# Moving the attention backward ahead of the gate and up weight gradients, with streamed operands and earlier end work, in a one-core transformer-block gradient kernel

## Chip, cores and metric

One core of one Trainium2 chip. The metric is the device time of one execution in microseconds (us); lower is better. A ratio is the mean time of one kernel's fast runs over that of the other's fast runs of the same rounds on the same chip, so it is not quite the ratio of the medians that are also quoted. A difference counts as faster or slower when its 95% interval lies outside 2%.

Two kinds of number are used: the timed runs (several executions of each kernel), and one profiled execution of each kernel, from which the stages are read. Profiled times are called spans. Engines: PE is TensorE's matmuls, PEld its weight loads, DVE is VectorE, ACT is ScalarE, POOL is GpSimd, SP issues the loads.

## The reference

The kernel computes the output of a transformer block and all its gradients in one pass. S = 2048 tokens, D = 512, 32 heads of 16, F = 1792, all bf16.

```python
def _A_ref(x, wqkv, wo):            # sliding local attention, window 8, dilation 2
    qkv = ...                        # (x @ wqkv) split into q, k, v by heads
    idx = pos[:, None] - arange(8)[None, :] * 2
    logits = einsum('bhsd,bhswd->bhsw', q, k[idx]) * scale   # masked where idx < 0
    attn = softmax(logits)
    o = einsum('bhsw,bhswd->bhsd', attn, v[idx])
    return o @ wo

def _B_ref(x, w_gate, w_up, w_down):
    return ((x @ w_gate) * (x @ w_up)) @ w_down

mod = silu(c) @ w_mod                # six rows of 512: sa, ca, ga, sb, cb, gb
h = layernorm(x) * (1 + ca) + sa
x = x + ga * _A_ref(h, A_wqkv, A_wo)
h = layernorm(x) * (1 + cb) + sb
x = x + gb * _B_ref(h, w_gate, w_up, w_down)
# outputs: x and the vjp of it for a given grad_out:
#          dx, dwqkv, dwo, dw_gate, dw_up, dw_down, dc, dw_mod
```

## The kernel before

The kernel walks through the block forward and then backward, one stage after the other. Two large buffers (BIG1, BIG2) and two of medium size (M1, M2) are handed from stage to stage; small work tiles come in numbered families `wt(0)` to `wt(5)` with four buffers each. Accumulators come from PSUM pools psA (2), psB (4) and psT (2). All loads are issued on one queue, all stores on another. A scheduler chooses each engine's instruction order from the program. Names: h1 and h2 are the outputs of the two layer norms, dao is the gradient of the attention block's output, oT the attention output before wo (transposed) and d_oT its gradient; dwmod(n) is one of six parts of dw_mod. Only what the change touches is shown.

```python
def store(out_ap, in_ap): nc.gpsimd.dma_start(out=out_ap, in_=in_ap)
def load(out_ap, in_ap):  nc.sync.dma_start(out=out_ap, in_=in_ap)

# --- start: x, the weights, then c; mod = silu(c) @ w_mod; weights are transposed and stored
for q in range(4):
    load(x_tok[:, q * 4:(q + 1) * 4, :], x_dram[:, q * 4:(q + 1) * 4, :])
# ... cut: loads of w_mod, wqkv, w_gate, w_up, w_down, wo
c_bf = sm(0, "c_bf", (P, DC), BF16)
nc.sync.dma_start(out=c_bf[:], in_=c.rearrange("o (dc p) -> p (o dc)", p=P))
# ... cut

def dwmod_chunk(n):                  # one 512x512 part of dw_mod: an outer product
    dmrow = wt(1, "dmrow")
    nc.vector.tensor_copy(out=dmrow[0:1, :], in_=dmodb[0:1, n, :])
    dwm_sb = wbig("dwm_sb")
    dwm3 = dwm_sb[:].rearrange("p (a b) -> p a b", a=DC)
    for dt in range(DC):
        ps = ps_tile(psB, "dwm_ps")
        nc.tensor.matmul(ps[:], lhsT=silu_row[0:1, dt * P:(dt + 1) * P], rhs=dmrow[0:1, :], start=True, stop=True)
        evac(dwm3[:, dt, :], ps[:], eng="s")
    store(out8_v[:, :, n * D:(n + 1) * D], dwm3)

# ... cut: forward, dw_down, dhh, then "dh" with norm-backward 2, which stores dao tile by tile
for n in (2, 3, 4, 5):
    dwmod_chunk(n)

# --- "dw": dw_gate and dw_up, h2 resident (2 MB)
h2_tok = _carve(m1, 0, [NT, D])
load(h2_tok, h2_d[:])
for XT, out_ap in ((DGT, out_4), (DUT, out_5)):
    for fq in range(4):
        fw = min(512, F - fq * 512)          # 512, 512, 512, 256
        nblk = fw // P
        accs = [ps_tile(psB, f"dw_acc{i}") for i in range(3)]
        accs.append(ps_tile(psA, "dw_acc3"))
        for t in range(NT):
            stg = pst_tile([P, 4, P], "stg")
            for j in range(nblk):
                nc.tensor.transpose(out=stg[:, j, :], in_=XT[:, fq * 4 + j, t * P:(t + 1) * P], identity=ident[:])
            stg_sb = wt(3, "stg_sb6", (P, 4, P))
            evac(stg_sb[:, 0:nblk, :], stg[:, 0:nblk, :], eng="v")
            rhs = stg_sb[:, 0:nblk, :].rearrange("p a b -> p (a b)")
            for dt in range(DC):
                nc.tensor.matmul(accs[dt][:, 0:fw], lhsT=h2_tok[:, t, dt * P:(dt + 1) * P], rhs=rhs, start=(t == 0), stop=(t == NT - 1))
        # ... cut: accumulators to SBUF, store

# --- "d_oT": dao transposed, times woT
load(dao_tok, dao_d[:])                      # 2 MB in one load
for t in range(NT):
    transpose_tok_to_T(dao_tok[:, t, :], d_aoT, t)
load(WoT, WoT_d[:])
# ... cut: 64 matmuls into do_ps, copied to d_oT (in BIG1)
# --- "dwo": oT and dao resident, 16 tiles of 4 transposes and 4 matmuls
# --- "dAT": attention weights' gradient; q, k, v resident in BIG2
for half in range(2):
    for htpair in range(2):
        for sc2 in range(2):
            ps = ps_tile(psB, "dat_ps")
            for htlo in range(2):
                for w in range(W):
                    prod = wt(0, "prodA")
                    ew.mul(prod[:], d_oT[...], vT2[...])          # VectorE
                    nc.tensor.matmul(ps[:], lhsT=GselP[:, htlo, w, :], rhs=prod[:], ...)
            evac(dAT[...], ps[:])
    # ... cut: softmax backward on VectorE, 8 tiles
# --- transposes of attention and its gradient (taT_ps), then the "dqkv loop", then:
h1_tok2 = _carve(big1, 0, [NT, D])
wmod2 = _carve(big1, NT * D, [DC, 6 * D])
load(h1_tok2, h1_d[:])                                        # 2 MB
load(wmod2, w_mod.rearrange("(dc p) n -> p dc n", p=P))       # 3 MB
# --- norm-backward 1
for t in range(NT):
    x_l = wt(4, "x_l9")
    load(x_l[:], x_dram[:, t, :])
    dx1_l = wt(5, "dx1_l9")
    load(dx1_l[:], dx1_d[:, t, :])
    # ... cut: dh1, layer norm backward (n_bwd is its first op on x), dx
# --- "dwq": dwqkv, 3 x 16 tiles of 4 transposes (psA) and 4 matmuls (psB)
# ... cut
for n in (0, 1):
    dwmod_chunk(n)
for dc in range(DC):
    nc.vector.tensor_tensor_reduce(out=junk10, in0=wmod2[:, dc, :], in1=dmod_rep, op0=ALU.mult, op1=ALU.add, scale=1.0, scalar=0.0, accum_out=dsilu[:, dc:dc + 1])
# ... cut: dc
```

## Time and profile before

Median 1368.64 us over 6 runs (1364.48 to 1372.37). The profiled execution has a span of 1370.7 us.

The busy line of the profile's page: for each engine the busy us, its share of the span and its instructions.

```profile
...
PE 1129.6 (82%) x5892; PEld 524.5 (38%) x5892; DVE 812.0 (59%) x2217; ACT 557.4 (41%) x1039; POOL 127.6 (9%) x243
...
```

TensorE is the busiest engine, but no engine is busy throughout. The stages follow one another, and each has its own limit. So the question is where TensorE starves. Busy time of each engine in four stretches of the kernel before (window, its length, busy us and instructions of each engine, granted TensorE clock as a share of full speed, DMA share, GB/s):

```profile
core 0: us, PE busy (x) PEld busy (x) DVE busy (x) ACT busy (x) POOL busy (x), PEclk, DMA share, GB/s
755.00:778.00 23.00, 16.80 (x49) 5.61 (x49) 8.12 (x22) 11.63 (x23) 3.35 (x5) 0.55 0.40 144
923.00:933.30 10.30, 0.11 (x2) 0.00 (x0) 0.00 (x0) 1.08 (x4) 0.75 (x1) 0.74 0.91 330
954.00:975.00 21.00, 20.91 (x141) 10.42 (x139) 11.15 (x31) 1.31 (x4) 0.18 (x2) 1.00 0.01 1
977.00:1035.00 58.00, 41.88 (x153) 13.88 (x152) 56.81 (x169) 5.22 (x9) 0.75 (x1) 0.81 0.07 26
...
```

The first stretch is the passage from dh to dw: TensorE is busy 16.80 of 23 us, and its granted clock is 0.55. The second is a stop: TensorE does 0.11 us in 10.3, while the DMA moves 330 GB/s. The third is dwo, with VectorE about half busy. The fourth is dAT with softmax backward: VectorE is busy 56.81 of 58 us.

What the stop waits for stands in the timeline of TensorE of the kernel before (start, busy us, instruction, then in brackets the idle time before it and what ended it):

```profile
...
933.36 3.24 PE L349 MATMUL stg<-ident,m_dao 128*128 128x128 bf16 x24 [10.25 <-DMA m_dao<-dao_d]
...
```

It is the single 2 MB load of dao. Two more waits, from the views of waits of the kernel before (engine, line and tile, what it waited for, total us, times, longest), the first at the start, the second at the start of norm-backward 1:

```profile
...
DVE t L84 <- DMA WgT_d<-wTt: 28.8, 1, 28.8
...
```

```profile
...
ACT n_bwd L627 <- DMA x_l<-in_A_x_dram: 11.3, 1, 11.3
...
```

The layer-norm products t cannot be written until the stored weight transposes have left their shared buffers. And norm-backward 1 waits for its first x tile, because 5 MB (h1 and w_mod) stand in front of it in the load queue.

At the end, the reductions for dc are four long VectorE operations. They are seen in the groups of VectorE instructions of the kernel before from 1289.8 us on (shapes, count | busy us, mean ns | idle):

```profile
...
L916 DVE CUSTOM_DVE_ANT_0 m_p<-big_p,m_p 128x3072 bf16<-128x3072 bf16 x4 | 13.3, 3336 | 0.0
...
```

Where they fall inside dwq, VectorE cannot copy the transposed tiles for TensorE. The waits of that stage, 1289.8 to 1357.0 us:

```profile
...
PE dwq_acc L901 <- DVE stg_sb L62: 12.8, 22, 1.6
...
```

### The profile page before, as it was taken

Reading aid. Unit: us, or ns where it says so; the run is one execution under the profiler, and the core shown is the slowest. Engines: PE = TensorE matmul, PEld = TensorE weight load, DVE = VectorE, ACT = ScalarE, POOL = GpSimd, SP = SyncE. Lnnn points to the kernel's source line nnn. Section 1 sums busy time; section 2 is a strip of 40 time slices with the busy share of each in tenths; the row PEclk is TensorE's granted clock in tenths of the full one; section 3 lists DMA queues with packets and bytes.
Section 4 is the critical chain, followed back from the end, with each engine's and each line's share of the span. In section 5 each row is a group of like instructions: output and inputs, shape, how many; then the busy total and the mean of one; then the engine's idle time right before and its main releaser. Section 6 shows DMA issues by size and latency. Waiting matters only on the chain. (4 is left out here: it accounts for less than half of the span.)

```text
span 1370.7 us, 16900 instructions
## 1 busy us (share of the span) xinstructions
PE 1129.6 (82%) x5892; PEld 524.5 (38%) x5892; DVE 812.0 (59%) x2217; ACT 557.4 (41%) x1039; POOL 127.6 (9%) x243
## 2 busy tenths in 40 slices
PE   1669959975999968798999788887977999978776
PEld 1334423332444434443444345454324334333343
DVE  1445879998445655484444323223796999955751
ACT  1833356751332111163444310112107888857602
POOL 4530000021000130000111100000000000001100
PEclk9858979986999989998999799998978999989998
DMA  9530320053113250203322303213101000042101
GB/s 363 150 116 31 126 95 14 1 215 123 39 35 97 69 188 24 66 1 127 97 93 83 125 32 122 104 50 127 47 0 47 1 1 1 0 177 92 55 16 62
DMA packets 58439, 110.10 MB, mean 80 GB/s; under 512 B 21360, under 2 KB 44400, under 8 KB 56176
## 3 DMA queue, kind: packets, MB, share of 16 engines
q1 hardware_dynamic: 45376, 62.24, 13.5%
q0 software_dynamic: 12976, 46.77, 9.2%
q8 instruction: 46, 0.75, 0.2%
q14 instruction: 41, 0.34, 0.1%
HBM read 62.23 MB, written 46.76 MB: 80 GB/s over the span
## 5 line engine op out<-in xcount | busy, mean ns | idle before, releaser
L62 DVE COPY stg_sb<-stg 128x512 bf16<-128x512 bf16 (+1 forms) x248 | 90.1, 401 | 201.2 <-PE stg L696 102.4
L701 PE MATMUL dw_acc<-stg_sb,m_h2tok 128*128 128x512 bf16 (+1 forms) x512 | 110.1, 357 | 19.9 <-DVE stg_sb L62 17.9
L60 ACT ACTIVATE arep_sb<-arep_ps 128x512 bf16<-128x512 f32 x128 | 76.6, 598 | 13.9 <-PE arep_ps L827 8.9
L701 PEld LDWEIGHTS <-m_h2tok 128*128 128x128 bf16 x512 | 49.7, 98 | 68.7 <-issue 27.1
L60 ACT ACTIVATE dlrep_sb<-dlrep_ps 128x512 bf16<-128x512 f32 x112 | 67.2, 600 | 8.2 <-PE dlrep_ps L831 3.9
L62 DVE CAST big_u<-gu_ps 128x512 bf16<-128x512 f32 x56 | 38.7, 692 | 52.9 <-PE gu_ps L521 52.9
L60 ACT ACTIVATE dw_sb<-dw_acc 128x512 bf16<-128x512 f32 (+1 forms) x32 | 14.8, 550 | 133.6 <-issue 116.0
L312 PE MATMUL stg<-ident,big_p 128*128 128x128 bf16 x232 | 31.5, 289 | 45.2 <-DMA big_p<-in_A_wqkv_dram 20.8
L580 PE MATMUL dwd_ps<-m_dffn,stg_sb 128*128 128x512 bf16 x224 | 55.0, 390 | 14.0 <-DVE stg_sb L62 14.0
L60 ACT ACTIVATE big_g<-gu_ps 128x512 bf16<-128x512 f32 x56 | 33.4, 597 | 69.6 <-PE gu_ps L521 69.6
L657 PE MATMUL dh_ps<-m_wgT,big_u 128*128 128x512 bf16 x224 | 56.2, 394 | 6.6 <-DMA m_wgT<-WgT_d 6.6
L84 DVE TENSOR_TENSOR Pq<-dlrep_sb,big_qkv 128x512 bf16<-128x512 bf16 x128 | 54.2, 424 | 11.1 <-ACT dlrep_sb L60 9.1
L84 DVE TENSOR_TENSOR Yv<-arep_sb,big_p 128x512 bf16<-128x512 bf16 x128 | 53.6, 418 | 11.0 <-ACT arep_sb L60 10.9
L521 PE MATMUL gu_ps<-m_h2T,wgb 128*128 128x512 bf16 x224 | 59.2, 388 | 0.8 <-DVE rstd L337 0.8
L521 PE MATMUL gu_ps<-m_h2T,wub 128*128 128x512 bf16 x224 | 58.9, 387 | 0.0
L382 PE MATMUL qkv_ps<-big_p 128*128 128x512 bf16 x192 | 55.6, 404 | 3.4 <-DVE big_p L62 2.1
L901 PE MATMUL dwq_acc<-stg_sb,big_p 128*128 128x512 bf16 x192 | 45.7, 378 | 14.4 <-DVE stg_sb L62 14.4
L659 PE MATMUL dh_ps<-m_wuT,big_g 128*128 128x512 bf16 x224 | 55.6, 379 | 0.0
L827 PE MATMUL arep_ps<-m_p,RepSel 128*128 128x512 bf16 x128 | 48.8, 381 | 7.4 <-ACT arep_sb L60 7.4
L60 ACT ACTIVATE rep_sb<-rep_ps 128x512 bf16<-128x512 f32 x86 | 47.0, 596 | 19.3 <-PE rep_ps L466 19.2
L84 DVE TENSOR_TENSOR prodL<-big_qkv 128x512 bf16<-128x512 bf16 x128 | 43.3, 420 | 19.2 <-PE lt_ps L400 15.0
L466 PE MATMUL rep_ps<-big_p,RepSel 128*128 128x512 bf16 x128 | 49.2, 388 | 5.9 <-ACT rep_sb L60 1.6
(234 smaller groups left out, 2303.0 us busy)
## 6 DMA issues: line engine op xcount, KB each, us to landing
qkvT_d<-big_qkv POOLq DMA_DIRECT2D x3, 2080.0 KB, 7.5
big_qkv<-qkvT_d SPq DMA_DIRECT2D x3, 2080.0 KB, 13.6
big_p<-in_w_mod_dram SPq DMA_DIRECT2D x2, 3072.0 KB, 14.5
x_l<-x_d SPq DMA_DIRECT2D x32, 128.0 KB, 2.4
out_dram<-dwm_sb POOLq DMA_DIRECT2D x6, 512.0 KB, 3.3
out_dram<-dw_sb POOLq DMA_DIRECT2D x6, 512.0 KB, 3.3
m_x<-in_A_x_dram SPq DMA_DIRECT2D x4, 512.0 KB, 5.5
h_d<-m_h POOLq DMA_DIRECT2D x4, 512.0 KB, 2.9
```

What stands on the lines that cost most here:

```text
L60: nc.scalar.activation(out=out, in_=in_, func=ACT.Copy)
L62: nc.vector.tensor_copy(out=out, in_=in_)
L84: self.eng(force).tensor_tensor(out=out, in0=in0, in1=in1, op=op)
L382: nc.tensor.matmul(ps[:], lhsT=W1[:, dc, ft * P:(ft + 1) * P], rhs=h1T[:, dc, sc * 512:(sc + 1) * 512], start=(dc == 0), stop=(dc == DC - 1))
L466: nc.tensor.matmul(rep_ps[:], lhsT=RepSel[:, htlo, w, :], rhs=attnT[:, htpair, sc * 512:(sc + 1) * 512], start=True, stop=True)
L521: nc.tensor.matmul(ps[:], lhsT=Wb[:, dc, :], rhs=h2T[:, dc, sc * 512:(sc + 1) * 512], start=(dc == 0), stop=(dc == DC - 1))
L580: nc.tensor.matmul(dwd_ps[:], lhsT=stg_sb[:, tt, :], rhs=d_ffn_tok[:, t, :], start=(t == 0), stop=(t == NT - 1))
L657: nc.tensor.matmul(dh2_ps[:], lhsT=DGT[:, fc, t * P:(t + 1) * P], rhs=WgT[:, fc, :], start=(fc == 0), stop=False)
L659: nc.tensor.matmul(dh2_ps[:], lhsT=DUT[:, fc, t * P:(t + 1) * P], rhs=WuT[:, fc, :], start=False, stop=(fc == FC - 1))
L701: nc.tensor.matmul(accs[dt][:, 0:fw], lhsT=h2_tok[:, t, dt * P:(dt + 1) * P], rhs=rhs, start=(t == 0), stop=(t == NT - 1))
L827: nc.tensor.matmul(arep_ps[:], lhsT=RepSel[:, htlo, w, :], rhs=attnT2[:, htpair, s0:s0 + 512], start=True, stop=True)
L901: nc.tensor.matmul(accs[dt][:], lhsT=h1_tok2[:, t, dt * P:(dt + 1) * P], rhs=rhs, start=(t == 0), stop=(t == NT - 1))
```

## The change

Its intent: fill the starved places with work that is ready, and take loads out of each other's way. It has three parts.

- A, start: the tiny load of c goes first, so that mod can be computed before the weight transposes.
- B, reorder: d_oT and dwo/dAT come right after dh, and dw after them. To make that fit in memory, h2, dao, oT, v, q, k and the attention tiles are no longer resident; they are streamed in 16 to 128 loads each. dw takes its four accumulators all from psB.
- C, end: h1 is loaded before the dqkv loop (BIG1 is free by then thanks to B); w_mod is loaded in two parts behind the first x tiles; dwmod(0, 1) moves ahead of dwq; four reductions over 3072 columns become four over 2048 and four over 1024.

```diff
+    c_bf = sm(0, "c_bf", (P, DC), BF16)                      # A: moved up, ahead of x
+        nc.sync.dma_start(out=c_bf[:], in_=c.rearrange("o (dc p) -> p (o dc)", p=P))
...
     for n in (2, 3, 4, 5):
         dwmod_chunk(n)
-    h2_tok = _carve(m1, 0, [NT, D])
-    load(h2_tok, h2_d[:])
+    for t in range(NT):                                      # B: d_oT moves here
+        dao_l = wt(4, "dao_l7")
+        load(dao_l[:], dao_d[:, t, :])
+        transpose_tok_to_T(dao_l[:], d_aoT, t, eng="v")
+    WoT_w = work.tile([P, DC * D], BF16, name="WoT_w", tag="wot", bufs=1)
+    # ... cut: d_oT matmuls, into psA
+    # ... cut: dAT loop, v streamed per (ht, sc); after each dAT group:
+                for t in range(2):
+                    dwo_tile((half * 4 + htpair * 2 + sc2) * 2 + t)
+    # ... cut: softmax backward, attention tiles streamed (a_l)
     for XT, out_ap in ((DGT, out_4), (DUT, out_5)):
-            accs = [ps_tile(psB, f"dw_acc{i}") for i in range(3)]
-            accs.append(ps_tile(psA, "dw_acc3"))
+            accs = [ps_tile(psB, f"dw_acc{i}") for i in range(4)]
             for t in range(NT):
+                h2_l = wt(4, "h2_l")
+                load(h2_l[:], h2_d[:, t, :])
...
+            a_l = wt(1, "a_l8c", (P, H * W))                 # B: transposes of attention
+            load(a_l[:], attn_d[:, t, :])
...
+    load(h1_tok2, h1_d[:])                                   # C: before the dqkv loop
...
-                Pk = wt(4, "Pk")
+                Pk = wt(2, "Pk")                             # shares its buffers with Yv
...
-    load(h1_tok2, h1_d[:])
-    load(wmod2, w_mod.rearrange("(dc p) n -> p dc n", p=P))
+    load(wmodB, w_mod.rearrange("(dc p) n -> p dc n", p=P)[:, :, 2 * D:6 * D])
...
+    for n in (0, 1):                                         # C: ahead of dwq
+        dwmod_chunk(n, pst=True)
+    load(wmodA, w_mod.rearrange("(dc p) n -> p dc n", p=P)[:, :, 0:2 * D])
...
+            if fq == 1 and t % 4 == 3:
+                dc = t // 4
+                nc.vector.tensor_tensor_reduce(out=wmodB[:, dc, :], in0=wmodB[:, dc, :], in1=dmod_repB, ...)
-    for n in (0, 1):
-        dwmod_chunk(n)
-        nc.vector.tensor_tensor_reduce(out=junk10, in0=wmod2[:, dc, :], in1=dmod_rep, ...)
+        nc.vector.tensor_tensor_reduce(out=junkA, in0=wmodA[:, dc, :], in1=dmod_repA, ...)
```

## The prediction

> **What bounds it now.** The page's busy table gives TensorE 82%, VectorE 59%, ScalarE 41%. Timeline and windows show where TensorE starves (us from the start):
> 1. 20–85: weight transposes. The layer-norm products t2 share buffers with the stored transposes: VectorE waits 28.8 us, until 84.6. c is loaded last (issued at 30.4), so 24 mod matmuls run at 42.8–50.7 among the transposes.
> 2. 755–778: TensorE busy 16.8 of 23 us, granted clock 0.55.
> 3. 923–933: waits 10.2 us for one 2 MB load of dao.
> 4. 954–1033: during dwo (954–975) VectorE is half busy (11 of 19 us); then dAT and softmax-backward, VectorE busy 56.8 of 58 us. Its work: 128 prodA at a pace of 0.337 us (43), 16 softmax tiles at 1.32 (21), 16 copies (6): 70 of 79 us.
> 5. 1218–1229: the first norm-backward tile waits 11.3 us for an x load queued behind h1 and w_mod (5 MB). The Trainium skill, "DMA: Bandwidth & Descriptors", section "Queues, rings and completion order", says each engine consumes descriptors in ring order; this trace agrees.
> 6. 1357–1371: dwmod after the last matmul group.
>
> **What changes, costed.** The built order shows the same matmuls:
> - Start: mod matmuls precede the transposes. These took 0.8 us per group (40 in 32.6 us); uninterrupted, t2 starts 4 us earlier, net of c's issue. Gain 4 (0 to 7).
> - d_aoT/d_oT (20.7 us, 933–954) moves to 755, into the low-clock gap, fed by 128 KB loads; wait 3 goes. d_oT done near 785. dAT with dwo alternating stays VectorE-bound: 71–75 us, to 859.
> - dw: old 149 us. New: 128 loads of 128 KB through four buffers. Full tiles take 1.31 us and comparable loads land in 2.3: hidden. Half-width groups (0.76 us per tile, 32 tiles) are tight: +2 to 6. Four accumulators now fill their pool, formerly 3+1 with a spare each: +0.5 us per boundary. About 158, to 1017.
> - Attention transposes: about 10 us as before (risk: attn loads queue behind h1's). dqkv starts near 1029 instead of 1042: gain 13 (3 to 22).
> - dqkv (1042–1213, TensorE, VectorE, ScalarE near 90%): same work; Pk and Yv share four buffers: loss 1–2.
> - Norm-backward 1: h1 loaded earlier, w_mod behind three x loads: 11.3 us go, nearly certain.
> - End: dwmod moves ahead of dwq (3 us of TensorE), saving 6 us of tail; four 3.3 us VectorE reductions become eight shorter ones, so TensorE waits less on copies (11.3 us in 1300–1371): net 5.
>
> Nearly all is on the critical path: the stages follow one another.
>
> **Predicted: 1337 us (-2.3%), 8 in 10 between 1322 and 1353.** Faster by over 2% 0.60, within 2% 0.39, slower by over 2% 0.01.
>
> **What would show the steps right.** The wait for x before the first n_bwd under 2 us; no 10 us wait for dao; dAT stage 71–76 us, VectorE over 90% busy, dwo inside it; dw 152–162 us, waits on h2 loads only in half-width groups; dqkv 171–174 us.
>
> **What would make it wrong.** h2 loads too slow, so dw is paced by DMA throughout: no gain. TensorE's fixed order stalling dAT behind dwo (oT loads have 256-byte rows). A cold clock prolonging d_oT: the skill's "TensorE: Matmul & The Clock Gate", Part 1, says idleness throttles it, and 0.55 at 755–778 agrees. Or no boundary loss in dw and d_oT hidden better: 1325.

## The result and the profile after

The changed kernel: median 1340.33 us over 8 runs (1336.65 to 1344.94). Before, in the same rounds: 1367.75 us over 16 runs (1363.75 to 1372.37). Ratio 0.9802, 95% interval 0.9785 to 0.9818: about 27 us less, with an interval that holds 2%. All outputs are right.

The first profiles of the two kernels differ by 36.4 us (spans 1370.7 and 1334.3), more than the times do. Both kernels were therefore profiled again (two more profiles of after, one more of before; e9, e10 and e11 below). The table has the stages of all five. "x to y" means from the last matmul of x, or the first instruction of a stage, as the trace gives it.

| stage, us | before | before again | after | after again | after again |
|---|---|---|---|---|---|
| start to end of dh | 754.2 | 749.6 | 747.5 | 749.3 | 747.4 |
| end of dh to first dqkv product (the reordered part) | 288.6 | 287.8 | 279.9 | 283.2 | 282.5 |
| dqkv loop | 169.2 | 167.8 | 168.7 | 168.7 | 169.1 |
| norm-backward 1 | 77.8 | 77.6 | 64.8 | 64.8 | 64.8 |
| dwq | 67.2 | 67.2 | 65.5 | 65.5 | 65.5 |
| tail | 13.7 | 13.7 | 7.9 | 7.9 | 7.9 |
| span | 1370.7 | 1363.7 | 1334.3 | 1339.4 | 1337.2 |

By the means of these columns, 30.2 us went: 3.8 before the end of dh, 6.3 in the reordered part, 12.9 in norm-backward 1, 1.7 in dwq and 5.8 in the tail; the dqkv loop gained nothing (0.3 us longer). The largest single gain is at the end of the kernel, not in the reorder.

Inside the reordered part, after: d_oT 36.4, dAT with dwo 73.5, dw 157.2, transposes 12.8 us. In the two repeats: 36.5 and 36.8, 73.5 and 73.4, 157.7 and 157.1, 15.5 and 15.2. The lines that answer to those of before follow. First the busy line of the page of after:

```profile
...
PE 1123.0 (84%) x5892; PEld 521.0 (39%) x5892; DVE 812.6 (61%) x2226; ACT 555.1 (42%) x1037; POOL 128.5 (10%) x243
...
```

The busy time of each engine in the d_oT, dAT and dw stages of after:

```profile
core 0: us, PE busy (x) PEld busy (x) DVE busy (x) ACT busy (x) POOL busy (x), PEclk, DMA share, GB/s
747.50:783.90 36.40, 32.03 (x164) 13.25 (x163) 13.88 (x38) 20.29 (x38) 4.10 (x6) 0.86 0.57 171
783.90:857.40 73.50, 57.46 (x275) 23.58 (x273) 67.79 (x199) 7.57 (x14) 0.75 (x1) 0.90 0.35 94
857.40:1014.60 157.20, 136.21 (x962) 77.72 (x963) 45.85 (x132) 13.60 (x28) 5.46 (x9) 0.98 0.43 130
...
```

The stop for dao is gone. In the dAT stage VectorE is busy 67.79 of 73.5 us, 92%, with dwo inside it. But the d_oT stage has a clock of 0.86 and TensorE is busy 32.03 us in it. What it does there, by groups of TensorE instructions in that window of after:

```profile
...
L699 PE MATMUL do_ps<-m_daoT,WoT_w 128*128 128x512 bf16 x64 | 18.3, 425 | 0.0
L349 PE MATMUL stg<-ident,dao_l 128*128 128x128 bf16 x64 | 7.1, 237 | 3.8 <-DMA dao_l<-dao_d 2.4 <-DVE prodga L84 1.4
L305 PE MATMUL dwm_ps<-dmrow,silu_row 1*128 1x512 bf16 x16 | 7.0, 464 | 0.0
...
```

The third line is 16 matmuls of dwmod, 7.0 us at a mean of 464 ns. The same 16 stood in the same passage in the kernel before. There they took 620 ns each, as the groups of before from 754.2 to 785 us show:

```profile
...
L305 PE MATMUL dwm_ps<-dmrow,silu_row 1*128 1x512 bf16 x16 | 7.7, 620 | 0.0
...
```

The wait for x at the start of norm-backward 1 (11.3 us before) has no line any more in the waits of after there. The split reductions of after from 1260.9 us on:

```profile
...
L920 DVE CUSTOM_DVE_ANT_0 m_wmodB<-m_wmodB,m_wmodA 128x2048 bf16<-128x2048 bf16 x4 | 9.1, 2279 | 0.0
L931 DVE CUSTOM_DVE_ANT_0 m_wmodA<-m_wmodA 128x1024 bf16<-128x1024 bf16 x4 | 4.9, 1215 | 0.0
...
```

And TensorE's waits for copies in dwq, 1260.9 to 1326.4 us of after, 7.5 us where they were 12.8:

```profile
...
PE dwq_acc L917 <- DVE stg_sb L62: 7.5, 20, 1.1
...
```

Now the costs. In dw of after, 859 to 1015 us, the groups of matmuls (full-width and half-width) and the waits on the streamed h2 (the profile calls the tile h_l):

```profile
...
L778 PE MATMUL dw_acc<-stg_sb,h_l 128*128 128x512 bf16 x384 | 93.2, 383 | 14.6 <-DVE stg_sb L62 13.5 <-DMA h_l<-h_d 1.0
...
L778 PE MATMUL dw_acc<-stg_sb,h_l 128*128 128x256 bf16 x128 | 17.9, 273 | 4.7 <-DMA h_l<-h_d 4.0 <-ACT dw_sb L60 0.4
...
```

```profile
...
PEld L778 <- DMA h_l<-h_d: 7.8, 12, 1.7
PE dw_acc L778 <- DMA h_l<-h_d: 4.9, 6, 1.5
...
PE dw_acc L778 <- ACT dw_sb L60: 0.4, 1, 0.4
...
```

The stream costs 12.7 us of waits, TensorE's and its weight loads' together (the two can overlap). 4.0 of the 5.0 us of matmul waits are in the half-width groups. Handing all four accumulators back to one pool costs 0.4 us in all. And the attention transposes of after, 1014.6 to 1029 us, wait for their streamed tiles:

```profile
...
PEld L804 <- DMA a_l8c<-attn_d: 4.7, 6, 1.6
...
PE taT_ps L804 <- DMA a_l8c<-attn_d: 2.4, 4, 1.3
...
```

### The profile page after: what moved, and what is told of

Its sections match the earlier page's. It is cut to its first block, busy times and chain, and to the rows that moved or that the text cites. A ratio compares the mean times of both kernels' runs of the same rounds, so it can differ in the third digit from the quotient of the medians.

```text
span 1334.3 us, 17557 instructions
## 1 busy us (share of the span) xinstructions
PE 1123.0 (84%) x5892; PEld 521.0 (39%) x5892; DVE 812.6 (61%) x2226; ACT 555.1 (42%) x1037; POOL 128.5 (10%) x243
## 4 chain that ended last, share of the span: by engine, by line
PE 38%; issue 31%; DVE 20%; ACT 4%; DMA 4%; POOL 3%; POOLq 0%; DVEq 0%; SPq 0%; ACTq 0%
PE gu_ps L521 8%; PE dw_acc L778 6%; PE dwd_ps L580 4%; PE dhh_ps L598 4%; PE qkv_ps L382 3%; DVE prodO L84 3%; PE dat_ps L733 3%; DVE stg_sb L62 2%; DVE rep_sb L62 2%; DVE prodL L84 1%; DVE st L332 1%; PE do_ps L699 1%; PE lt_ps L400 1%; PE dwo_acc L719 1%; PE stg L349 1%
## 5 line engine op out<-in xcount | busy, mean ns | idle before, releaser
L778 PE MATMUL dw_acc<-stg_sb,h_l 128*128 128x512 bf16 (+1 forms) x512 | 111.1, 356 | 19.2 <-DVE stg_sb L62 13.5
L778 PEld LDWEIGHTS <-h_l 128*128 128x128 bf16 x512 | 48.0, 98 | 64.1 <-issue 21.6
L84 DVE TENSOR_TENSOR Pq<-dlrep_sb,k_l 128x512 bf16<-128x512 bf16 x128 | 54.2, 424 | 18.4 <-ACT dlrep_sb L60 16.0
L60 ACT ACTIVATE big_g<-gu_ps 128x512 bf16<-128x512 f32 x56 | 33.4, 597 | 70.1 <-PE gu_ps L521 70.1
L84 DVE TENSOR_TENSOR Yv<-arep_sb,m_doT 128x512 bf16<-128x512 bf16 x128 | 53.6, 419 | 9.4 <-ACT arep_sb L60 9.4
L917 PE MATMUL dwq_acc<-stg_sb,big_p7b 128*128 128x512 bf16 x192 | 47.4, 379 | 9.3 <-DVE stg_sb L62 9.2
L837 PE MATMUL arep_ps<-big_p7b,RepSel 128*128 128x512 bf16 x128 | 48.4, 378 | 7.2 <-ACT arep_sb L60 6.5
L84 DVE TENSOR_TENSOR Pk<-dlrep_sb,q_l 128x512 bf16<-128x512 bf16 x128 | 53.5, 418 | 0.0
```

The source lines that it names most:

```text
L60: nc.scalar.activation(out=out, in_=in_, func=ACT.Copy)
L84: self.eng(force).tensor_tensor(out=out, in0=in0, in1=in1, op=op)
L778: nc.tensor.matmul(accs[dt][:, 0:fw], lhsT=h2_l[:, dt * P:(dt + 1) * P], rhs=rhs, start=(t == 0), stop=(t == NT - 1))
L837: nc.tensor.matmul(arep_ps[:], lhsT=RepSel[:, htlo, w, :], rhs=attnT2[:, htpair, s0:s0 + 512], start=True, stop=True)
```

## The experiments

Twelve runs were made: eight new kernels, and four repeats to see the scatter. The theory: the gain is a sum of separate waits removed, and about half of it needs no reorder at all; the reorder itself gains little, because it brings three losses with it (d_oT carries the dwmod matmuls at a low clock; h2 loads in the half-width groups; attention tiles behind the h1 load). The rival: the gain comes from the reorder, and the rest follows from it. The first four kernels put one part of the change alone into the kernel before. They were timed together on one chip, five rounds; the kernel before had a median of 1367.01 us over 11 runs there.

### e1_c_early: part A alone

```diff
# the kernel before, plus:
+    c_bf = sm(0, "c_bf", (P, DC), BF16)
+    nc.sync.dma_start(out=c_bf[:], in_=...)      # moved ahead of the x loads
     m1 = new_m1("m1_x")
```

> The kernel before with one part of the change alone: the tiny load of c moved to the front of the load queue. My theory: the 24 mod matmuls run before the weight transposes (they ran at 42.8 to 50.7 us), so the first layer-norm product, which waits for the transposes' buffers, starts 2 to 4 us earlier (84.8 us before, 82.7 in the changed kernel), and the whole is 2 to 5 us faster: ratio 0.996 to 0.9985. Rival: c's 2 us of issue delays all 12 MB of loads behind it and the transposes are paced by their stores, so the start gains nothing: ratio 1.000 within 0.001, and what the two profiles differ by there is run-to-run variation.

Measured: 1365.95 us, ratio 0.9987 (0.9969 to 1.0005). The interval holds 1, so the times do not show a gain. The traces do, a small one: the first layer-norm product t starts at 84.0 to 84.9 us in the four profiles with c late (before twice, e2, e3; mean 84.5), and at 81.2 to 83.9 us in the ten with c early (mean 82.6). That is 1.9 us, where the prediction had 4. The traces also show what the prediction left out. With mod ahead of them the weight transposes are no longer interrupted and take 53.3 us in e1 (26.4 to 79.7) instead of 62.5 in before (20.8 to 83.3), but they start 5.6 us later. The wait of t on their buffers even grew, from 28.8 to 54.0 us, because it began sooner; only its end counts.

### e2_loads_late: only the end's load queue

```diff
# the kernel before, with:
-    load(h1_tok2, h1_d[:])
-    load(wmod2, w_mod.rearrange("(dc p) n -> p dc n", p=P))
     for t in range(NT):
         x_l = wt(4, "x_l9")
         ...
+        if t == 3:
+            load(h1_tok2, h1_d[:])
+            load(wmod2, w_mod.rearrange("(dc p) n -> p dc n", p=P))
```

> The kernel before with the 3 MB load of w_mod issued behind four of the x loads of the last norm-backward loop instead of ahead of all of them; the built order still puts the 2 MB load of h1 ahead. Queue theory: the 11.3 us wait of the first norm tile is the time that 5 MB take to drain ahead of a 128 KB load; with 2 MB ahead it shrinks in proportion, to 1 to 4 us, and the whole gains 7 to 10 us: ratio 0.993 to 0.995. Rival: the x loads come late because their buffers (shared with the products of the stage before) come free late, so the wait stays at 10 us or more and the ratio is 1.000 within 0.001.

Measured: 1360.51 us, ratio 0.9945 (0.993 to 0.996), 7.5 us less. In the built order only w_mod went behind the x loads; the scheduler kept h1 in front. So this became a dose test: 5 MB in front of x before, 2 MB here, none in after. The wait for x in the same place of e2's waits:

```profile
...
ACT n_bwd L627 <- DMA x_l<-in_A_x_dram: 3.7, 1, 3.7
...
```

The wait is 11.3, 3.7 and 0 us for 5, 2 and 0 MB, and norm-backward 1 takes 77.8, 70.1 and 64.8 us. That is 7.7 us for 3 MB and 5.3 us for 2 MB, about 2.6 us per MB both times. For the 3 MB the queue order is shown to be the cause, since e2 changes nothing else; from e2 to after more than the order changes, so the 5.3 us fit it but do not show it alone. The Trainium skill, "DMA: Bandwidth & Descriptors", section "Queues, rings and completion order", says that an engine consumes the descriptors of a ring in order; this trace agrees, with those numbers. The stage shrinks by 13.0 us in all, while the one wait that the prediction counted was 11.3; the other 1.7 us were not traced to a single wait.

### e3_dwm_early: dwmod(0, 1) ahead of dwq

```diff
# the kernel before, with:
     nc.vector.tensor_copy(out=dmodb[:, 1, :], in_=dca_ps[:])
+    for n in (0, 1):
+        dwmod_chunk(n, pst=True)                 # accumulator from psT
     ...
-    for n in (0, 1):
-        dwmod_chunk(n)
```

> The kernel before with the two dwmod chunks moved from behind the last weight-gradient group to ahead of it, with their accumulators in the transposes' pool. My theory: the tail after the last matmul of that group shrinks from 13.3 us to about 7.5 us, paid for by 2 to 3 us of matmuls earlier, so the gain is 3 to 4 us: ratio about 0.9975. Rival: the chunks share two accumulators with the transposes and stall them, so what the tail gains is lost in the loop: ratio 1.000 within 0.001.

Measured: 1365.09 us, ratio 0.9982 (0.9965 to 0.9998), 2.5 us less. The profile shows both sides: the tail after the last dwq matmul goes from 13.7 to 7.9 us, and the dwq stage grows from 67.2 to 69.6 us. Net 3.4 us by the stages; the times agree within their interval. The tail of 7.9 us is that of after.

### e4_all_but_reorder: e1, e2 and e3 together

> The three edits above in one kernel: everything of the change that does not need the reordering of the attention-backward and gate/up-gradient stages. If the gains add: 2 to 5, 7 to 10 and 3 to 4 us, together 12 to 19 us, ratio 0.986 to 0.991. The changed kernel as a whole is at 0.980, so the reordering itself with its streamed loads would be worth 8 to 15 us. Rival, from the lengths of stages in the two profiles: the reordering itself (from the end of the second norm-backward to the start of the dq/dk/dv loop, 287.8 us against 281) is worth 7 us or less, and nearly all of the 27 us come from the other parts: ratio 0.983 or lower here.

The edit is the three diffs above in one kernel. Measured: 1353.48 us, ratio 0.9897 (0.9882 to 0.9912), 14 us less; the three alone sum to 11.8, so they add within their intervals. About half of the change's 27 us thus needs no reorder. The rival of this section (the gain comes from the reorder) falls as it was stated, and so does the ratio of 0.983 or lower that this run's own rival expected. What is left to the reorder and to what only it allows (h1 loaded before the loop, and the split reductions, which were kept with it) is 13 us by the ratios 0.9897 and 0.9802. By the stages it is 7.5 us in the reordered part (six profiles with the old order have 287.8 to 290.7 us, mean 289.4; three of after 279.9 to 283.2, mean 281.9), 5.4 us in norm-backward 1 (70.2 to 64.8) and 4.1 us in dwq (69.6 to 65.5). No kernel has the reorder alone, so its own worth is an estimate: 7.5 us by the stages; 13 − 5.4 − 4.1 = 3.5 us by the times. That gap, 4 us, is not settled.

The next four kernels start from the changed kernel and attack the three losses one by one. They were timed together, five rounds; before had a median of 1365.54 us over 9 runs. The changed kernel was not timed in these rounds, so it is compared through the ratios to before.

### e5_attn_early: the attention tiles loaded during dw

```diff
# the changed kernel, with:
+    big2 = new_big2("big2_dqkv")                  # moved up; its last quarter is free
+    dqkvT = _carve(big2, 0, [3, DC, S])
+    attn_r = _carve(big2, 3 * DC * S, [NT, H * W])
+    for q in range(4):
+        load(attn_r[:, q * 4:(q + 1) * 4, :], attn_d[:, q * 4:(q + 1) * 4, :])
     for sc in range(NCH):                         # transposes
-            a_l = wt(1, "a_l8c", (P, H * W))
-            load(a_l[:], attn_d[:, t, :])
-            ... in_=a_l[:, htpair * P:(htpair + 1) * P]
+            ... in_=attn_r[:, t, htpair * P:(htpair + 1) * P]
```

> The changed kernel with the attention weights for the transposes loaded in the middle of the gate/up-gradient stage into a free part of the large buffer, instead of 16 small loads that queue behind the 2 MB load of h1. Theory: the transposes stage took about 14 us (1015 to 1029) instead of 10 because these small loads landed late; with the data present it takes 10 us or less and the whole gains 3 to 5 us on the changed kernel: ratio to before 0.9765 to 0.978. Rival: the stage is paced by the eight 1.02 us evictions and the cold clock, so it stays at 13 to 14 us: ratio 0.980 within 0.001.

Moving the h1 load later in the program was looked at first (no run shows it); it did not change the built order of the loads, so the attention tiles were moved instead. Measured: 1336.24 us, ratio 0.978 (0.9754 to 0.9806). The transposes take 9.6 us instead of 12.8 to 15.5, and the waits on attention tiles have no line any more. (dw, into which these loads moved, takes 158.8 us, 1.1 to 1.7 us longer.) By the times the gain over the change, 0.9802 to 0.978, is 3 us, within the intervals. The stage shows the loss; the times alone would not.

### e6_h2_deep: eight buffers for h2

```diff
# the changed kernel, with:
-                h2_l = wt(4, "h2_l")
+                h2_l = wt(4 + t % 2, "h2_l")
```

> The changed kernel with eight instead of four buffers for the streamed h2 tiles (two buffer groups in turn). Theory: the loads pace only the half-width groups, which took 13.7 and 14.4 us against 12.2 before; with eight buffers the waits for h2 loads (12.8 us in all on the matmul and weight-load queues) go, the stage falls from 155.8 to 150 to 152 us, and the whole gains 3 to 5 us: ratio to before 0.9765 to 0.978. Rival: the loss in the stage is at the borders between accumulator groups, with all four accumulators of one pool; then the stage stays at 154 us or more and the ratio at 0.980 within 0.001.

Measured: 1339.65 us, ratio 0.980 (0.9772 to 0.9827): no gain that the times show. (Here the h2 tiles alternate between two work families of four.) Yet dw itself is quicker, 153.0 us against 157.2, as it should be when the half-width groups no longer wait on h2: the loss is real, and 4 us. Part of it was given back in the next stage, where the transposes take 16.8 us (12.8, 15.5 and 15.2 us in the three profiles of after). The waits of e6 on the attention tiles there, 1018 to 1036 us:

```profile
...
PEld L804 <- DMA a_l8c<-attn_d: 8.2, 5, 4.2
...
PE taT_ps L804 <- DMA a_l8c<-attn_d: 5.6, 3, 3.1
...
```

In after these were 4.7 and 2.4 us, in its repeats 6.4 to 6.5 and 3.2 us. In the built order of e6 the q, k and h1 loads stand ahead of the attention tiles, in after only h1. So 1.3 to 4.0 us of the gain went into a longer wait on the same queue, depending on the profile it is compared with. dw and transposes together take 169.8 us here and 169.0 in e12, against 170.0, 173.2 and 172.3 in the profiles of after: how much of the 4 us is kept stays open. e6's profile also had a d_oT stage of 40.9 us, where the code is that of after (36.4); this was tested again as e12.

### e7_dwm_mid: dwmod(2..5) into the dAT loop

```diff
# the changed kernel, with:
-    for n in (2, 3, 4, 5):
-        dwmod_chunk(n)
     ...
                 evac(dAT[:, htpair, sc2 * 512:(sc2 + 1) * 512], ps[:], eng="s")
+                if sc2 == 0:
+                    dwmod_chunk(2 + half * 2 + htpair, pst=True)
```

> The changed kernel with the four dwmod chunks (16 matmuls, 16 evictions) moved out of the stage that makes d_oT into the stage after it, where VectorE is the limit and TensorE is busy 58 of 75 us. Theory: they lengthen the first stage (36.4 us from the last matmul of norm-backward to the last of d_oT, 30 predicted) at a low clock and cost nothing in the second: first stage 29 to 32 us, second unchanged at 73 to 75, gain 4 to 7 us, ratio to before 0.975 to 0.977. Rival: the first stage is set by the chain of the last tile (norm, store, load, transpose) and stays at 35 us or more, or the chunks take transposes' accumulators in the second stage and lengthen it by as much: ratio 0.980 within 0.0015.

Measured: 1332.4 us, ratio 0.9756 (0.9733 to 0.978): faster than before, and by the ratios (0.9802 and 0.9756) 6 us better than the change. The d_oT and dAT stages of e7 by windows:

```profile
core 0: us, PE busy (x) PEld busy (x) DVE busy (x) ACT busy (x) POOL busy (x), PEclk, DMA share, GB/s
746.10:774.60 28.50, 23.16 (x133) 11.02 (x132) 12.52 (x34) 12.72 (x23) 1.08 (x2) 0.88 0.43 126
774.60:851.90 77.30, 61.40 (x305) 24.81 (x303) 69.51 (x204) 16.24 (x29) 3.79 (x5) 0.88 0.44 124
...
```

d_oT falls from 36.4 to 28.5 us and dAT rises from 73.5 to 77.3: net 4.1 us. TensorE had room in dAT, where VectorE sets the pace. Of the dwmod matmuls one is still in d_oT; the others are inside dAT.

The 7.9 us by which d_oT falls are a little more than TensorE's 7.0 us of dwmod, and the clock fits this. The windows of e7 where the clock was low:

```profile
core 0: us, PE busy (x) PEld busy (x) DVE busy (x) ACT busy (x) POOL busy (x), PEclk, DMA share, GB/s
758.00:760.00 2.00, 0.92 (x8) 0.77 (x8) 0.42 (x2) 0.19 (x1) 0.00 (x0) 0.74 0.77 234
760.00:762.00 2.00, 1.75 (x9) 0.67 (x8) 1.38 (x5) 0.45 (x1) 0.00 (x0) 0.50 0.67 184
762.00:764.00 2.00, 2.00 (x6) 0.65 (x5) 0.00 (x0) 0.73 (x2) 0.00 (x0) 0.50 0.66 178
764.00:766.00 2.00, 2.00 (x7) 0.75 (x6) 0.00 (x0) 0.61 (x2) 0.00 (x0) 0.56 0.08 23
766.00:768.00 2.00, 2.00 (x11) 0.94 (x10) 0.00 (x0) 1.19 (x2) 0.00 (x0) 1.00 0.00 0
...
```

The clock is at half for about 6.8 us and comes back while the d_oT matmuls run. In after it is at half from about 760 to 770 us, while dwmod, transposes and d_oT matmuls alternate.

### e8_combined: e5, e6 and e7 together

> The three edits above to the changed kernel together. If each of the three losses was real and separate, the gains add to 10 to 16 us: ratio to before 0.968 to 0.973. If they share one cause (the cold clock, or the load queue), the sum is less than the largest two: ratio above 0.974.

The edit is the three diffs above in one kernel. Measured: 1326.45 us, ratio 0.9703 (0.9677 to 0.9729). It beats both kernels, before by 3.0% and the change by about 1%, and it is the version to keep. From the end of dh to the first dqkv product it takes 269.1 us (281.9 in after): d_oT 28.6, dAT 77.3, dw 153.6, transposes 9.6. With the attention tiles already there, the eight h2 buffers keep their 4 us. By the ratios, e5, e6 and e7 alone gain 3, 0 and 6 us over the change and together 13.5; the excess fits e6's gain no longer turning into a wait, though the intervals are too wide to prove it.

### e9_after_again and e10_after_again2: the changed kernel profiled twice more

No edit.

> The changed kernel unchanged, profiled again, to see how far one profile of it stands for its timed runs. Theory (the d_oT stage between the end of dh and the end of d_o differs from one execution to the next with the granted clock, 36.4 us at 0.86 in the profile on record and 40.9 us at 0.75 in that of the deeper h2 buffers, same code there): this stage 36 to 41 us, its granted clock between 0.75 and 0.86 and the longer the lower; every other stage within 1.5 us of the profile on record (dAT stage 73.5, dw 157, transposes 12.8, loop 168.7, norm-backward 1 64.8, dwq 65.5, tail 7.9); span 1334 to 1343. Rival (the profile on record was quicker everywhere by a per cent or so): all stages longer by 0.3 to 0.5 %, the d_oT stage at 36.4 to 36.6 us.

> The same again: theory, d_oT stage 36 to 41 us and following the granted clock of that stage, the others within 1.5 us of the profile on record; rival, all stages longer by 0.3 to 0.5 % alike. Span 1334 to 1343.

Measured: 1341.07 and 1338.86 us (single runs, state unknown), spans 1339.4 and 1337.2. Neither reading holds as written. The d_oT stage took 36.5 and 36.8 us at a clock of 0.86, so it is not what varied; nor was every stage longer by the same share. What differs is the start (up to 1.8 us at the end of dh) and the transposes (15.5 and 15.2 us against 12.8), which wait for loads; all other stages agree within 0.5 us. The first profile of after was quicker than its repeats by 3 to 5 us.

### e11_before_again and e12_h2_deep_again

No edit: the kernel before, and e6's kernel, once more.

> The kernel before, unchanged, profiled again: how far its one profile stands for its timed runs. The two repeats of the changed kernel agreed with its first profile within 0.5 us in every stage but two, both with load waits: the start (up to 1.8 us later at the end of dh) and the attention transposes (15.2 and 15.5 us against 12.8). Theory (the same holds of before: only stages that wait for loads differ): start to end of dh 750 to 754.5, from there to the first Pq 288 to 291, loop 169, norm-backward 1 77 to 78, dwq 67, tail 13.7; span 1364 to 1371. Rival (before's profile on record was slow everywhere): all stages shorter by 0.3 %.

> The kernel with eight h2 buffers, profiled again. Its first profile had 40.9 us from the end of dh to the end of d_o, where four profiles of kernels with the same code there had 36.4 to 36.8. Chance: 36.4 to 37 this time, span 1338 to 1340. Deeper h2 buffers delaying the loads of that stage by the order of the queue or the engines' programs: 40 to 41 again, span 1341 to 1343. Both: dw 153 us and transposes 16 to 18 us again.

Measured, e11: 1365.37 us, span 1363.7. The stages from norm-backward 1 on agree within 0.2 us with the first profile; the end of dh is 4.6 us earlier and the dqkv loop 1.4 us shorter, so not only load waits vary. The first profile of before was thus a slow one; that and the quick first profile of after account for a difference of 36 us between them when the times differ by 27.

Measured, e12: 1334.69 us (single run), span 1332.6. The d_oT stage is back at 36.5 us, so the 40.9 of e6 was chance. dw is 153.2 us, so that finding of e6 held; the transposes' 15.8 us are within 0.6 us of the repeats of after, so the new wait is hardly more than scatter. What the chance was is visible in the clock. e6, windows from 760 us:

```profile
core 0: us, PE busy (x) PEld busy (x) DVE busy (x) ACT busy (x) POOL busy (x), PEclk, DMA share, GB/s
760.00:764.00 4.00, 4.00 (x17) 1.56 (x14) 2.43 (x8) 1.66 (x4) 0.00 (x0) 0.51 0.88 243
764.00:768.00 4.00, 4.00 (x18) 1.52 (x17) 1.95 (x6) 2.76 (x6) 0.76 (x1) 0.50 0.46 156
768.00:772.00 4.00, 4.00 (x12) 0.97 (x11) 1.17 (x4) 0.60 (x1) 0.76 (x1) 0.50 0.88 272
772.00:776.00 4.00, 4.00 (x10) 1.28 (x10) 0.00 (x0) 1.87 (x4) 0.00 (x0) 0.50 0.27 81
776.00:778.00 2.00, 2.00 (x6) 0.43 (x4) 0.00 (x0) 1.68 (x4) 0.42 (x1) 0.71 0.01 4
...
```

TensorE is busy in every microsecond of this, and the clock stays at one half for some 17 us; in after this lasted 10. The timeline has dwmod matmuls, one contraction row each, spread over 762.3 to 772.9 us here; the clock rises only after ten d_oT matmuls in a row (772.8 to 777.2). The kernel before, profiled again, shows the opposite edge:

```profile
core 0: us, PE busy (x) PEld busy (x) DVE busy (x) ACT busy (x) POOL busy (x), PEclk, DMA share, GB/s
756.00:758.00 2.00, 1.87 (x10) 0.98 (x9) 2.00 (x6) 0.00 (x0) 0.75 (x2) 0.50 0.56 197
758.00:760.00 2.00, 2.00 (x11) 0.67 (x9) 1.37 (x6) 0.77 (x2) 0.00 (x0) 0.79 0.03 8
760.00:762.00 2.00, 2.00 (x13) 0.81 (x13) 0.00 (x0) 2.00 (x5) 0.41 (x1) 1.00 0.00 0
762.00:764.00 2.00, 1.89 (x5) 0.39 (x4) 0.00 (x0) 1.26 (x3) 0.80 (x2) 0.56 0.54 190
...
```

Here the clock had come back at about 759 us. Then dwmod matmuls made up most of TensorE's work from 758.8 to 763.9 us, TensorE was 100% busy, and the clock fell to half again at about 762 us.

Both stretches hold transposes (128x128) as well as one-row matmuls, so either could be what does not raise the clock. Traces at hand separate the two. In e1, TensorE ran nothing but dwmod matmuls from 765.4 to 768.8 us, busy 3.28 of 3.4 us: the clock was at half and was still there in the 3.4 us after. In before, from 1033.75 to 1037.15 us, it ran transposes but for one matmul, busy 3.14 of 3.4 us at half, and had the full clock in the 3.4 us after. All changes of the clock in these traces lie multiples of 3.41 us apart. Cut into such stretches, the fourteen traces have 2562 in which TensorE was busy for over 3.2 us without any dwmod matmul, and none of these was followed by half clock; of 63 with dwmod matmuls, 25 were. So the one-row matmuls are what these stretches have in common, though no run was made to test it.

## Why the prediction was right, and where its terms were off

The prediction was 1337 us with a range of 1322 to 1353; the median was 1340.33. Its chain of stages was right and nearly every mechanism it named was found. By terms:

- Start, predicted 4 us (0 to 7): measured 1.9 us in the start of the layer-norm products over fourteen profiles. Over-sized by half: it counted that the transposes run uninterrupted (53.3 instead of 62.5 us in e1), but not that with mod in front they start 5.6 us later.
- d_oT to 785, about 30 us: measured 36.4. This is the mis-sized term of the reorder. It costed the d_oT matmuls and their loads, but left out the 16 dwmod matmuls, 7.0 us, that run in the same passage in both kernels, and which the profile of before already showed at 620 ns each. 36.4 − 7.0 is 29.4; with them moved (e7) the stage took 28.5 us. The prediction had named a cold clock prolonging d_oT as a way to be wrong, and the stage's clock was 0.86; but with dwmod moved out the stage met its 30 us at 0.88, so the uncounted matmuls are the larger part of it. Its reason for the low clock, idleness, holds for the beginning only: in before the clock fell at 757.2 us during 3.45 us of idle time, but from 764.1 to 770.9 us TensorE was busy in all 6.80 us, mostly with dwmod, and the clock was still 0.50.
- dAT, predicted 71 to 75 us, VectorE-bound over 90%: measured 73.5 us, 92%. Right. The 10 us wait for dao is gone as predicted.
- dw, predicted about 158 us (152 to 162), with waits mainly in half-width groups: measured 157.2. Right in sum. Its parts were not quite: accumulator boundaries were put at 0.5 us each and cost 0.4 us in all. Of the 8 us over the old 149, deeper buffers for h2 (e6) give back 4. The starts of the matmuls place most of the rest at the beginning of the stage: 1.6 us pass before its first accumulating matmul, and its first accumulator group takes 22.9 us where the other full-width groups take 20.9 to 21.5 (20.8 to 21.0 in before). What causes this was not tested.
- Transposes, about 10 us with the risk that their loads queue behind h1: measured 12.8 to 15.5. The risk was what happened; e5 shows it by taking it away (9.6 us).
- dqkv loop, 1 to 2 us lost to shared buffers: measured 0.3 us, within the scatter. No loss.
- Norm-backward 1, 11.3 us: measured 12.9 to 13.0, and proportional to the bytes in front of x (e2). Right, under-sized by 1.7 us.
- End, net 5 us: measured 5.8 in the tail and 1.7 in dwq, 7.5 us. The reductions gained more than thought: waits on copies fell from 12.8 to 7.5 us, although 2.4 us of dwmod came in.

So the reordered part gained 7.5 us rather than the 13 predicted, and the end gained about 20 rather than 16. The errors partly cancelled, so that the total came so near is in part luck. With the stages' sums as measured, 1.9 + 7.5 − 0.3 + 12.9 + 7.5 = 29.5 us, against 27 us timed; the difference of 2 to 3 us lies within the scatter of single profiles.

What stays open: the reorder's own worth (3.5 or 7.5 us, see e4); whether one-row matmuls really keep the clock down, to which the traces point but which no run isolates; and which of the two halves of e7's timed gain of 6 us (moved work, 4.1 us by the stages; the rest) is more than scatter.

## What to carry to other kernels

When a reorder moves a stage into a gap, list everything else that already runs in that gap, with its measured durations: here 16 small matmuls that nobody had counted cost 7 us of the gain. Every load taken out of a crowded place goes somewhere else in the same queue, so read the built order for what it now stands ahead of; a gain in one stage (e6) can in part become a wait in the next until that is cleared too (e8). And test the cheap parts alone: half of this large change's gain came from three edits of a few lines.

## What the Trainium skill lacked or had wrong

- "TensorE: Matmul & The Clock Gate", Part 1, "The HAM clock gate", gives full clock after one busy window of about 3.4 us. The two states it names agree with the records (0.50 and 1.00; 128x512 matmuls of about 379 ns at full clock, dwmod's at 620 ns when cold). But TensorE was busy without a break for 17 us in e6 with the clock at 0.50, and in e11 the clock fell from 1.00 to 0.50 while TensorE was 100% busy. Both times matmuls with a single contraction row (1x128 by 1x512) were a large part of the work. The page does not say whether such matmuls count as activity; these records suggest that busy time alone does not decide it: in e1 3.4 us of nothing else, busy 3.28 us, left the clock at 0.50, while in before 3.4 us of transposes but for one matmul, busy 3.14 us, were followed by 1.00. No run tested this by itself.
- "DMA: Bandwidth & Descriptors", "Queues, rings and completion order", gives the ring order without a size for its cost; the page's bandwidth figures stand in other sections and are not tied to it. Here 3 MB ahead in the queue delayed the stage behind them by 7.7 us, about 2.6 us per MB.
- No page read for this says how far one profile stands for a kernel. Here three profiles of one kernel had spans of 1334.3, 1339.4 and 1337.2 us, with most stages equal within 0.5 us and the difference in the start and in one stage that waits for loads.
